# A fused attention and token-mixing kernel on one core: a new written-out order for all five engines

## The chip, the cores and the metric

The kernel runs on one of the eight cores of a Trainium2 chip. A core has five engines that run side by side and meet through semaphores: TensorE (PE) multiplies matrices and writes into PSUM, ScalarE (ACT) and VectorE (DVE) do elementwise work and move results from PSUM to SBUF, GpSimd (POOL) does elementwise work in SBUF and issues DMAs, SyncE (SP) only issues DMAs. PSUM has eight banks per partition; this kernel sees them as four pairs. The metric is device microseconds of one execution, and the number given for a kernel is the median of its runs.

## The reference

Attention with a sliding window of 128 tokens and a bias that falls with distance, and behind it a token-mixing layer whose mixing weights are computed from the tokens themselves:

```python
scores = scale * np.matmul(q, k.transpose(0, 1, 3, 2))        # 8 batches, 8 heads, 576 tokens, 64 wide
mask = (rel >= 0) & (rel < window)
scores = np.where(mask, scores + bias[None], -1000000000.0)
attn = softmax(scores)
x = (attn @ v).transpose(0, 2, 1, 3).reshape(B, S, H * D)     # 8 x 576 x 512
wq = x @ w_q
wk = x @ w_k
W_tok = scale * np.einsum('bsd,btd->bst', wq, wk)
mixed = np.einsum('bst,btd->bsd', W_tok, x)
out = np.maximum(mixed, 0.0) @ w_out
```

## The kernel before

**Stages of a batch.** The kernel works through eight batches. For each batch, loads bring in q, k and v and turn them to 16 bits on the way (`Lq`, `Lk`, `Lv`, with `Lt` for the last 64 tokens of two batches together). TensorE transposes q and k (`TW` for batches 0 to 3, `TN` for 4 to 7, `TT` for the last tokens), and ACT or DVE copies each transposed block out of PSUM (`ETW`, `ETN`, `ETT`). Then follow, for four groups of keys and two halves of the heads each, the scores (`QK`), their exponential on ACT (`EXP`, 64 in all), and the multiplication by the precomputed exponential of bias and mask on DVE (`MUL`, 64 in all). `PV` multiplies by v, and `X` on DVE divides by the row sums (a reciprocal and a multiplication; 40 in all). The token mixing transposes x (`XT`, copied by `EXT`), projects it (`WQ`, `WK`, copied by `EWQ`, `EWK`), forms x transposed times wk (`G`, copied by `EG`), mixes (`MX`, copied through the ReLU by `RM`), and multiplies by w_out (`OUT`, copied by `EO`, stored by `DO`). `mixed` is computed as wq times (wk transposed times x), so no 576 by 576 matrix is formed.

**The order.** Nothing of the order follows from loops. The functions of the kernel only register operations with their dependencies. A string `ORDER` then lists all 773 operations, each with its engine: `QK0.2.0:P:1:5` stands for the scores of batch 0, group 2, half 0 on PE (`P`), in PSUM pair 1, behind 5 fill matmuls; a second digit of a bank names the half of the pair; `A`, `V`, `G` and `S` are ACT, DVE, POOL and SP. The loop at the end of the kernel (lines 861 to 876) emits the operations in that order. Each engine runs its own operations strictly in the order of the string, so what counts is the order within an engine; between engines, and for the reuse of a PSUM bank, semaphores make one wait for the other. A fill matmul computes nothing that is used; it multiplies a constant tile into a bank that the next operation overwrites.

**The load queue.** All loads but the first two run through POOL's queue, in which set-up work (`iota`, `mask`, `ident`, and memsets such as `ones`, `zerop`, `pads`) and part of the stores stand too. `load` (line 368) gives each load an estimated service time; before a load is issued, it waits for an earlier one to have landed, so that the estimated service of the loads under way stays within `AHEAD`, 6.0 us. `HOLD` marks a place in SP's list: the first store of SP behind it waits for the load that is the fourth from the last to have landed.

**What a PE operation waits for** can be read from the names: `TW` needs its loads and the permutation matrix `permh` (`perm`, made from `ident`); `QK` needs the copies of both transposes of its half; `PV` needs the `MUL` of its groups and its v; every one of them needs its bank to have been emptied by the copy behind the operation that had the bank before.

Of the kernel before, what the change touches and what calls it, by code (L numbers as in the profile page):

```python
# [44 lines left out]
ETT0:A MUL0.0.1:V QK0.3.0:P:1:2 ETT1:V EXP0.3.0:A Lv0.3:G PV0.0:P:2 MUL0.1.1:V QK0.3.1:P:3  # L45
X0.0:V ETW1.1.0:A Lv0.4:G PV0.2:P:1 ETW1.1.1:A Lk2.1:G MUL0.3.0:V PV0.1:P:2 EXP0.3.1:A
X0.2:V Lk2.0:G QK1.2.1:P:0 EXP1.2.1:A QK1.1.1:P:3 MUL0.3.1:V Lq2.1:G TW1.0:P:1:1 X0.1:V
EXP1.1.1:A Lq2.0:G PV0.3:P:0 ETW1.0.0:A MUL1.1.1:V Lwq:G QK1.3.1:P:2 ETW1.0.1:A X0.3:V
PV0.4:P:3 EXP1.3.1:A QK1.0.1:P:1 X0.4:V Lv1.0:G XT0.0:P:0 EXP1.0.1:A EXT0.0:V Lv1.1:G
XT0.2:P:20:2 QK1.2.0:P:3 QK1.0.0:P:1 EXT0.2:A MUL1.0.1:V EXP1.2.0:A XT0.1:P:0 Lwk:G  # L50
QK1.1.0:P:2 MUL1.3.1:V EXP1.0.0:A EXT0.1:V Lv1.2:G TW2.1:P:3 MUL1.2.0:V EXP1.1.0:A Lv1.3:G
MUL1.2.1:V QK1.3.0:P:0 ETW2.1.1:A TW2.0:P:1 MUL1.0.0:V Lt1.2:G ETW2.1.0:A wqq:V EXP1.3.0:A
Lv1.4:G MUL1.1.0:V WQ0.0:P:20 ETW2.0.0:V PV1.0:P:3 Lt1.3:G ETW2.0.1:A WQ0.1:P:21 X1.0:V
EWQ0.0:A Lt1.1:G QK2.1.1:P:0 EWQ0.1:A QK2.0.0:P:1 Lwo.0:G PV1.1:P:2 MUL1.3.0:V EXP2.0.0:A
WK0:P:30 Lt1.0:G X1.1:V EXP2.1.1:A WQ0.2:P:31 PV1.2:P:1 Lk3.0:G EWQ0.2:V QK2.1.0:P:2 EWK0:A
ones4:G X1.2:V PV1.3:P:0 EXP2.1.0:A QK2.0.1:P:3 Lq3.0:G X1.3:V PV1.4:P:1 EXP2.0.1:A
QK2.2.0:P:2 Lwo.1:G X1.4:V G0:P:00 EXP2.2.0:A Lwo.3:G XT1.0:P:3 ones2:G EG0:V XT1.2:P:01
XT1.1:P:1 EXT1.0:A EXT1.2:V QK2.2.1:P:2 EXT1.1:V TT1:P:0 Lwo.2:G MX0.0:P:3 ETT3:A MUL2.0.1:V
Lv2.0:G WQ1.1:P:10 ETT2:A EXP2.2.1:A RM0.0:V WK1:P:11 ones3:G EWQ1.1:V WQ1.0:P:01 RM0.2:A
EWK1:V QK2.3.0:P:2 EWQ1.0:A Lv2.1:G MUL2.2.0:V MX0.2:P:3 MX0.1:P:1 G1:P:00 RM0.4:A  # L60
MUL2.1.1:V RM0.3:A Lk3.1:G TW3.0:P:3 EXP2.3.0:A EG1:V Lv2.2:G MUL2.2.1:V QK2.3.1:P:0 RM0.1:A
MX1.0:P:2 ETW3.0.1:V Lq3.1:G EXP2.3.1:A MX1.1:P:1 MUL2.0.0:V OUT0.1:P:31 Lv2.4:G RM1.0:A
RM1.1:V Lv2.3:G PV2.0:P:0 RM1.3:A ETW3.0.0:V OUT0.0:P:20 RM1.2:A X2.0:V Lq4.0:G EO0.1:A
OUT0.2:P:10 EO0.0:A MUL2.1.0:V QK3.0.0:P:3 MUL2.3.1:V Lq4.1:G QK3.1.0:P:0 EO0.2:A PV2.1:P:2
MUL2.3.0:V EXP3.0.0:A Lv3.0:G OUT1.0:P:11 X2.1:V EXP3.1.0:A Lq4.2:G PV2.2:P:3 MUL3.0.0:V
TW3.1:P:2 EO1.0:A Lk4.3:G MUL3.1.0:V X2.2:V QK3.2.0:P:0 ETW3.1.0:A Lk4.1:G PV2.4:P:1
EXP3.2.0:A ETW3.1.1:V OUT0.3:P:20 Lk4.0:G X2.4:V QK3.2.1:P:3 Lk4.2:G QK3.0.1:P:0 EO0.3:V
EXP3.2.1:A PV2.3:P:1 Lq4.3:G OUT1.3:P:21 EXP3.0.1:A X2.3:V Lv3.1:G WQ1.2:P:20 QK3.3.1:P:3
EWQ1.2:A EO1.3:V QK3.3.0:P:1 EXP3.3.1:A XT2.1:P:0 Lt2.3:G MUL3.2.1:V OUT1.2:P:20 Lv3.2:G
EXP3.3.0:A EXT2.1:V XT2.2:P:21 XT2.0:P:3 MUL3.0.1:V TN4.0.0:P:0 Lv3.4:G EXT2.2:A EXT2.0:A  # L70
MX1.2:P:1 WQ2.1:P:21 ETN4.0.0:V Lv3.3:G RM1.4:A QK3.1.1:P:3 MUL3.2.0:V EWQ2.1:A TN4.1.0:P:1
EXP3.1.1:A PV3.0:P:0 Lt2.0:G MUL3.3.1:V OUT1.4:P:21 Lv4.0:G X3.0:V ETN4.1.0:A TN4.0.1:P:3
EO1.2:A TN4.1.1:P:1 MUL3.1.1:V Lq5.3:G QK4.0.1:P:0 ETN4.0.1:A WK2:P:20 EO1.4:V ETN4.1.1:A
Lt2.2:G PV3.1:P:3 EXP4.0.1:A MUL3.3.0:V Lq5.2:G QK4.0.0:P:1 X3.1:V WQ2.0:P:21 EXP4.0.0:A
# [18 lines left out]
Lv5.4:G MUL5.3.0:V WQ3.2:P:21 WQ4.0:P:30 EXP5.2.0:A Lk7.1:G EWQ3.2:V WQ4.1:P:31 EG4:V
EWQ4.0:V MX3.2:P:0 TN6.0.1:P:2 EWQ4.1:A Lk7.3:G TN6.1.1:P:1 RM3.4:V ETN6.0.1:A XT5.0:P:3
ETN6.1.1:V TT3:P:0 Lv6.2:G EXT5.0:A QK6.1.1:P:2 MUL5.2.0:V MX4.0:P:1 ETT6:A MX4.1:P:3
EXP6.1.1:A Lv7.3:G RM4.0:V OUT3.4:P:00 RM4.1:V RM4.3:A Lv6.1:G PV5.3:P:2 RM4.2:A MUL6.0.1:V
QK6.0.0:P:3 EO3.4:A Lv6.0:G PV5.2:P:1 X5.3:V ETT7:A OUT4.2:P:00 EXP6.0.0:A Lq7.2:G X5.2:V
QK6.1.0:P:2 Lq7.3:G QK6.2.1:P:3 MUL6.0.0:V EXP6.1.0:A TN7.1.0:P:1 OUT4.3:P:01 EO4.2:V
DO3.4:G EXP6.2.1:A ETN7.1.0:V PV5.4:P:2 MUL6.1.1:V QK6.3.0:P:1 EO4.3:A Lk7.2:G TN7.0.0:P:3
X5.4:V EXP6.3.0:A OUT4.1:P:00 Lv6.3:G MUL6.1.0:V ETN7.0.0:A QK6.3.1:P:2 XT5.1:P:1 MUL6.3.0:V  # L100
DO0.0:G EXP6.3.1:A QK6.2.0:P:3 OUT3.3:P:01 EO4.1:V Lv7.1:G EXT5.1:A MUL6.2.1:V PV6.0:P:2
EXP6.2.0:A DO2.2:G OUT4.0:P:00 X6.0:V Lv6.4:G EO3.3:A WQ5.1:P:10 MUL6.2.0:V EO4.0:A DO0.1:G
XT5.2:P:11 TN7.0.1:P:3 TN7.1.1:P:2 EWQ5.1:A EXT5.2:V QK7.0.0:P:0 ETN7.0.1:V DO2.3:G
ETN7.1.1:A PV6.2:P:1 MUL6.3.1:V EXP7.0.0:A DO1.0:G WQ5.0:P:30 X6.2:V PV6.1:P:2 Lv7.4:G
EWQ5.0:A QK7.1.1:P:0 QK7.1.0:P:3 X6.1:V Lv7.0:G EXP7.1.1:A WQ4.2:P:10 WK5:P:11 HOLD:S
EWQ4.2:V DO3.3:G PV6.4:P:2 EXP7.1.0:A EWK5:V QK7.2.0:P:0 DO1.1:G X6.4:V PV6.3:P:1 EXP7.2.0:A
DO0.3:G QK7.3.1:P:3 X6.3:V G5:P:20 EXP7.3.1:A DO4.2:G XT6.0:P:0 EG5:V DO1.2:G XT6.1:P:1
EXT6.0:A XT6.2:P:21 QK7.0.1:P:3 EXT6.1:V EXT6.2:A Lv7.2:G EXP7.0.1:A MX5.1:P:0 MX4.2:P:2
WQ6.0:P:10 RM5.3:V DO3.0:G WK6:P:11 RM5.1:A MUL7.3.1:V RM4.4:A WQ5.2:P:30 DO1.4:G
QK7.2.1:P:0 EWQ5.2:A MUL7.0.0:V MX5.0:P:2 EWK6:A QK7.3.0:P:3 EWQ6.0:V RM5.0:A G6:P:11  # L110
RM5.2:V DO3.2:G EXP7.3.0:A WQ6.1:P:10 MUL7.1.0:V DO2.0:G OUT5.2:P:20 EG6:A EWQ6.1:V
EXP7.2.1:A MUL7.1.1:V OUT5.3:P:21 MUL7.3.0:V EO5.2:A MX6.1:P:1 MUL7.2.0:V MX5.2:P:3
MX6.0:P:0 EO5.3:A OUT5.1:P:20 RM5.4:V RM6.1:A MUL7.0.1:V RM6.3:A PV7.4:P:3 MUL7.2.1:V
RM6.2:A PV7.1:P:1 EO5.1:A X7.4:V OUT5.0:P:21 RM6.0:A DO5.1:G X7.1:V PV7.0:P:3 PV7.3:P:0
EO5.0:A X7.0:V WQ6.2:P:20 PV7.2:P:1 DO5.0:S OUT6.2:P:21 X7.3:V DO2.1:S OUT6.1:P:30 DO1.3:S
X7.2:V EO6.2:A EWQ6.2:A XT7.2:P:31 XT7.0:P:0 DO6.2:S EO6.1:V EXT7.2:A XT7.1:P:1 MX6.2:P:2
# [793 lines left out]
```

## Time and profile before

| | us |
|---|---|
| median of 3 runs | 137.87 (137.78 to 138.77) |
| the profiled execution, span from the first to the last instruction | 137.4 |
| PE busy | 127.2 (93% of the span) |
| ACT busy | 113.8 (83%) |
| DVE busy | 112.0 (82%) |
| POOL busy | 105.3 (77%) |
| end of the last matmul | 132.45 |

The profiled execution has no time of its own beside its span; its span of 137.4 stands 0.5 below the median of the runs, which is what lies around it. Matmuls are pipelined: a row's duration runs until the result is in PSUM, and the next operation starts before that. So the cost of a PE operation is read from its start to the start of the next one.

### The profile page before, as it was taken

To read this page: it belongs to the slowest core of one execution; us is meant where nothing else is said; L and a number is where in the kernel's file an instruction comes from. 1 tells how busy PE (TensorE), PEld (TensorE's weight loads), DVE (VectorE), ACT (ScalarE), POOL (GpSimd) and SP (SyncE) were. 2 spreads that over 40 slices of the span, in tenths; PEclk is the share of its full clock that TensorE was granted. 3 is DMA by queue.
4 is the path that set the end of the run, shared out by engine and by line. 5 is a ranking of instruction groups with operands and counts; after the bars stand their busy time and mean duration, and the time that the engine had idled before them with its cause. 6 is when DMAs were issued, how large, how long until landed. Compare 5 with 4: busy or idle time off the path is not lost.

```text
span 137.4 us, 5570 instructions
## 1 busy us (share of the span) xinstructions
PE 127.2 (93%) x2364; PEld 83.5 (61%) x2364; DVE 112.0 (82%) x236; ACT 113.8 (83%) x187; POOL 105.3 (77%) x170
## 2 busy tenths in 40 slices
...
DMA packets 92680, 24.86 MB, mean 181 GB/s; under 512 B 80240, under 2 KB 89200, under 8 KB 92656
## 3 DMA queue, kind: packets, MB, share of 16 engines
...
q8 instruction: 18, 0.29, 0.8%
...
## 4 chain that ended last, share of the span: by engine, by line
PE 72%; ACT 8%; DMA 5%; POOL 5%; issue 3%; DVE 2%; POOLq 0%; DVEq 0%
PE pair L214 62%; PE pair L217 10%; DMA natw<-in_k_dram 5%; ACT pt L604 5%; POOL natt L220 2%; POOL natw L220 2%; ACT qkT L492 2%; DVE x L650 1%; DVE xtl L650 1%; DVE xT L237 1%; DVE inv L649 0%; ACT xT L235 0%; ACT osb L229 0%; ACT wqT L229 0%; POOL wm L293 0%
## 5 line engine op out<-in xcount | busy, mean ns | idle before, releaser
L604 ACT ACTIVATE pt<-pair 128x1024 f16<-128x1024 f32 x64 | 63.3, 1038 | 6.0 <-PE pair L214 5.8
L220 POOL DMA_DIRECT2D vt<-in_v_dram x40 | 36.5, 968 | 1.2 <-DMA natw<-in_k_dram 0.8
L611 DVE TENSOR_TENSOR pt<-pt,bias 128x1024 f16<-128x1024 f16 x48 | 32.2, 684 | 1.4 <-ACT pt L604 1.3
L214 PE MATMUL pair<-wout_sb,rm 128*128 128x512 f16 x128 | 32.0, 380 | 0.1
L223 POOL DMA_DIRECT2D out_dram<-natw x19 | 10.6, 566 | 19.5 <-DVE natw L231 10.9
L214 PEld LDWEIGHTS <-pt 128*128 128x128 f16 x576 | 21.2, 98 | 5.5 <-issue 2.2
L214 PE MATMUL pair<-qkT 64*128 64x256 f16 (+3 forms) x352 | 23.8, 247 | 0.4 <-ACT pt L604 0.3
L214 PE MATMUL pair<-vt,pt 128*128 128x65 f16 x576 | 23.8, 194 | 0.1
L220 POOL DMA_DIRECT2D natw<-in_k_dram x24 | 22.9, 993 | 1.2 <-POOLq L894 0.8
L220 POOL DMA_DIRECT2D natw<-in_q_dram x23 | 21.5, 989 | 2.0 <-DMA natw<-in_k_dram 0.7
L650 DVE TENSOR_TENSOR x<-pair,inv 128x512 f16<-128x512 f32 x32 | 22.1, 692 | 1.1
L214 PEld LDWEIGHTS <-rm 128*128 128x128 f16 x128 | 10.8, 97 | 10.9 <-issue 0.9
L214 PEld LDWEIGHTS <-qkT 64*128 64x128 f16 x352 | 11.9, 96 | 7.7 <-issue 3.9
L229 ACT COPY natw<-pair 128x512 f32<-128x512 f32 x24 | 14.1, 607 | 2.2 <-PE pair L214 2.1
L217 PEld LDWEIGHTS <-natw 128*64 128x64 f16 (+1 forms) x512 | 12.8, 103 | 4.8 <-issue 1.9
L214 PE MATMUL pair<-fill 128*128 128x512 f16 x28 | 10.4, 506 | 1.2 <-DVE fill L348 1.2
L750 ACT ACTIVATE rm<-pair 128x512 f16<-128x512 f32 x20 | 11.4, 611 | 0.0
L611 DVE TENSOR_TENSOR pt<-pt,biasl 128x1024 f16<-128x1024 f16 x16 | 10.9, 683 | 0.0
L217 PE MATMUL pair<-permh,natw 128*64 128x128 f16 x256 | 9.1, 223 | 1.8 <-DMA natw<-in_k_dram 1.4
L649 DVE RECIPROCAL inv<-pair 128x8 f32<-128x8 f32 (+1 forms) x40 | 8.1, 203 | 3.1 <-PE pair L214 2.3
L214 PE MATMUL pair<-xT,wqq_sb 128*128 128x256 f16 x64 | 9.3, 273 | 0.4 <-ACT qkT L492 0.4
L752 DVE TENSOR_SCALAR rm<-pair 128x512 f16<-128x512 f32 x12 | 7.9, 684 | 1.6 <-PE pair L214 1.6
...
## 6 DMA issues: line engine op xcount, KB each, us to landing
...
```

The lines of the kernel that those rows point to most:

```text
L214: hold(nc.tensor.matmul(*a, **k))
L217: hold(nc.tensor.transpose(*a))
L220: hold(nc.gpsimd.dma_start(**k))
L223: i = (nc.gpsimd if eng == "POOL" else nc.sync).dma_start(**k)
L229: hold(nc.scalar.copy(out_ap, in_ap))
L492: hold(nc.scalar.copy(dst, src))
L604: nc.scalar.activation(out=pt[:, 0:1024], in_=two(s.bank).rearrange("p e c -> p (e c)"), func=AF.Exp, scale=SCALE)
L611: nc.vector.tensor_tensor(out=pt[:, 0:1024], in0=pt[:, 0:1024], in1=bt, op=ALU.mult)
L649: nc.vector.reciprocal(out=inv[r], in_=pxv[r, :, :, 64])
L650: nc.vector.tensor_tensor(out=x[r].rearrange("p (g h d) -> p g h d", g=2, h=4), in0=pxv[r, :, :, 0:64], in1=inv[r].unsqueeze(3).broadcast_ ...
L750: hold(nc.scalar.activation(out=out_ap, in_=in_ap, func=AF.Relu, scale=WSCALE))
L752: hold(nc.vector.tensor_scalar(out=out_ap, in0=in_ap, scalar1=0.0, scalar2=WSCALE, op0=ALU.max, op1=ALU.mult))
```

## The change

Only the string `ORDER` differs. The same 773 operations stand in it. What differs:

- the order within every engine, from the first operation to the last;
- which of ACT and DVE does a copy out of PSUM: ACT has 5 `ETT` fewer, 2 `ETN` fewer, 2 short `EWQ` and 2 short `EXT` fewer, 3 `EXT`, 2 `EG`, 1 `EWK`, 1 `EWQ` and 1 `EO` more, and DVE the opposite;
- the memsets: `zerop`, `pads` and `ones4` move from POOL to DVE, `ones0` from DVE to POOL;
- the fill matmuls: 10 ahead of the first transposition, where there were 28 at eight places (12, 5, 1, 3, 2, 2, 1 and 2);
- the PSUM bank of most PE operations;
- the stores: POOL has 20 and SP 16, where each had 18, and `HOLD` stands three places before the end of the string.

The beginning and the end of the string, before (`-`) and after (`+`):

```diff
 ORDER = """
-FQ1:S ones1:V FQ0:S Lk0.0:G ones0:V iota:G Lq0.1:G dist:V mask:G Lk0.1:G bias1:A ident:G
-CQ0:V CQ1:A Lt0.2:G zeros:V bias0:A idh:V Lt0.1:G perm:V TW0.0:P:0:12 Lt0.0:G biasl0:V
-Lq1.1:G ETW0.0.1:A ETW0.0.0:V Lt0.3:G QK0.2.0:P:1:5 Lk1.1:G QK0.1.0:P:2 EXP0.2.0:A Lv0.0:G
-TW0.1:P:0:1 EXP0.1.0:A Lv0.2:G QK0.0.0:P:3 ETW0.1.1:V ETW0.1.0:A zerop:G MUL0.1.0:V
-EXP0.0.0:A QK0.2.1:P:1:3 QK0.0.1:P:2 QK0.1.1:P:0 MUL0.0.0:V Lv0.1:G EXP0.1.1:A TT0:P:3
-biasl1:V Lk1.0:G EXP0.2.1:A MUL0.2.0:V Lq1.0:G TW1.1:P:0:2 EXP0.0.1:A MUL0.2.1:V pads:G
...
-EO7.4:A OUT7.0:P:00 DO7.4:S EO7.1:V OUT7.3:P:01 DO7.1:G EO7.0:A OUT7.2:P:10 DO7.0:S EO7.3:A
-DO7.3:S EO7.2:A DO7.2:S
+FQ0:S FQ1:S zerop:V pads:V Lk0.1:G Lq0.1:G Lk0.0:G iota:G Lt0.2:G dist:V ones4:V Lq1.0:G mask:G
+bias1:A bias0:A ones0:G ident:G biasl1:V CQ1:A perm:V TW0.1:P:0:10 Lt0.3:G Lt0.1:G Lt0.0:G
+zeros:V CQ0:V TW0.0:P:1 ETW0.1.0:A ETW0.1.1:A QK0.1.1:P:0 EXP0.1.1:A QK0.0.1:P:2 QK0.2.1:P:3
+ETW0.0.1:V ETW0.0.0:V EXP0.0.1:A QK0.2.0:P:1 EXP0.2.0:A biasl0:V MUL0.1.1:V Lk1.0:G QK0.0.0:P:0
+EXP0.0.0:A QK0.1.0:P:2 EXP0.1.0:A Lv0.0:G EXP0.2.1:A ones1:V idh:V TT0:P:1 MUL0.0.1:V ETT0:V
+QK0.3.0:P:0 EXP0.3.0:A Lv0.1:G ETT1:V MUL0.2.0:V MUL0.1.0:V Lk1.1:G MUL0.0.0:V TW1.0:P:1
+QK0.3.1:P:2 PV0.0:P:3 X0.0:V PV0.1:P:0 Lq1.1:G ETW1.0.0:A ETW1.0.1:A QK1.2.0:P:1 QK1.0.0:P:3
...
+EXP2.1.0:A TW2.1:P:1 ETW2.1.1:V ETW2.1.0:A MUL1.3.0:V XT1.0:P:2 EXT1.0:A PV1.2:P:3 X1.2:V
...
+EXP2.2.0:A TW3.1:P:1 ETW3.1.0:A TT1:P:0 WQ1.2:P:20 ETT2:A MUL2.1.1:V MUL2.1.0:V MUL2.0.1:V
+ETW3.1.1:V MUL2.2.1:V MUL2.2.0:V MUL2.0.0:V EWQ1.2:V ETT3:V WK1:P:30 EWK1:A QK2.3.1:P:1
+EXP2.3.1:A QK2.3.0:P:3 EXP2.3.0:A MUL2.3.1:V G1:P:00 EG1:A QK3.0.1:P:1 EXP3.0.1:A TW3.0:P:2
...
+EO7.3:A DO7.4:S DO7.3:S OUT6.3:P:31 DO6.0:G EO7.1:A DO7.1:S OUT7.2:P:30 EO7.2:V EO6.3:A DO6.3:S
+DO7.2:S OUT6.2:P:20 EO6.2:V OUT7.0:P:31 EO7.0:A HOLD:S DO6.2:S DO7.0:S
 """
```

More of the change, by code (lines that the diff above doesn't have):

```diff
@@ L45 @@
[L45 to L74, printed above, removed]
@@ L93 @@
[L93 to L116, printed above, removed]
```

89 lines of the change are left out of this document (67 added, 22 removed).

## The prediction

> **What bounds the kernel now.** I read the page first, then the busy times in stretches of 10 us, then PE's timeline.
>
> ```profile
> span 137.4 us, 5570 instructions
> PE 127.2 (93%) x2364; PEld 83.5 (61%) x2364; DVE 112.0 (82%) x236; ACT 113.8 (83%) x187; POOL 105.3 (77%) x170
> PE 72%; ACT 8%; DMA 5%; POOL 5%; issue 3%; DVE 2%; POOLq 0%; DVEq 0%
> ```
>
> ```profile
> 10.00:20.00 10.00, 7.69 (x129) 4.56 (x124) 5.97 (x12) 6.73 (x10) 9.43 (x23) 0.84 1.77 165
> 20.00:30.00 10.00, 9.32 (x243) 7.51 (x244) 9.47 (x19) 9.99 (x15) 7.40 (x10) 0.99 1.59 165
> 40.00:50.00 10.00, 10.00 (x175) 6.51 (x173) 9.91 (x20) 9.85 (x17) 9.09 (x12) 1.00 1.90 156
> 120.00:130.00 10.00, 10.00 (x120) 5.53 (x118) 5.97 (x13) 5.33 (x13) 0.54 (x1) 1.00 0.94 340
> ```
>
> The columns of the second view are stretch, length, then busy time of PE, weight loads, DVE, ACT and POOL, and PE's granted clock, DMA share, GB/s. PE holds 72% of the chain of waits and is full from 40 us on, but DVE and ACT are nearly full beside it (9.91 and 9.85 of 10): three engines in balance. Slack exists only in the first 40 us and, for DVE and ACT, behind 120. To see what PE can still save I need the price of its operations, from start to next start:
>
> ```profile
> 42.24 1.06 PE L217 MATMUL pair<-permh,natw 128*64 128x128 f16 x32
> 43.24 0.41 PE L214 MATMUL pair<-qkT 64*128 64x128 f16 x12
> 43.48 0.74 PE L214 MATMUL pair<-wqT,gs 64*128 64x512 f16 x4
> 44.20 1.02 PE L214 MATMUL pair<-wout_sb,rm 128*128 128x512 f16 x4
> 45.06 0.42 PE L214 MATMUL pair<-vt,pt 128*128 128x65 f16 x8
> ...
> 128.83 3.62 PE L214 MATMUL pair<-wout_sb,rm 128*128 128x512 f16 x16
> ```
>
> A TW costs 43.24 - 42.24 = 1.00, a QK 0.24, an OUT 0.86, and so on; an operation behind one of another array tiling costs 0.10 more. These are PE's first rows from TW3.0 on and its last, the end, 128.83 + 3.62 = 132.45. With the median step of each kind between them, the 256 PE operations cost 112.9 us in the order of before (108 changes of tiling). So 132.45 - 112.9 = 19.6 us are lost. TW3.0 starts at 42.24 with 24.4 us of work ahead of it: 17.8 lost by then, 1.8 in the 90 us behind. **The change is decided by what PE loses before 44 us, and by whether the rest stays gapless.**
>
> **The change part by part.**
>
> *PE work.* In the new order the same sum is 112.5 us (111 changes of tiling, but fewer in front of costly kinds). 18 fills less save nothing: they stand where PE would wait. *ACT and DVE.* ACT hands eleven mostly short copies to DVE and takes eight longer ones: within 0.2 us on either engine; zerop, pads and ones4 run on DVE in its first 6 us, where it waits for the mask anyway.
>
> *The start.* These rows carry it:
>
> ```profile
> 1.28 0.90 POOL L220 DMA_DIRECT2D natw<-in_k_dram  x1 [0.83 <-POOLq L894]
> 4.28 1.33 ACT L305 ACTIVATE bias<-wm 128x256 f16<-128x256 f32 x4 [2.26 <-POOL wm L295]
> 5.36 0.29 POOL masks.py:199 TENSOR_SCALAR_AFFINE_SELECT ident<-ident 128x128 f32<-128x128 f32 x1
> 6.42 1.15 PE L217 MATMUL pair<-permh,natw 128*64 128x128 f16 x32
> 7.66 0.80 POOL L220 DMA_DIRECT2D natw<-in_q_dram  x1
> 8.69 0.63 PE L214 MATMUL pair<-qkT 64*128 64x256 f16 x8
> 9.14 1.94 ACT L604 ACTIVATE pt<-pair 128x1024 f16<-128x1024 f32 x2 [0.93 <-PE pair L214]
> 11.62 1.00 POOL L336 MEMSET pt<- 128x64 f16 x10
> 15.25 1.01 POOL L340 MEMSET xtl<- 128x512 f16 x2
> 16.29 1.03 PE L217 MATMUL pair<-permh,natw 128*64 128x128 f16 x24 [1.40 <-DMA natw<-in_k_dram]
> 18.87 1.02 ACT L604 ACTIVATE pt<-pair 128x1024 f16<-128x1024 f32 x1 [3.18 <-PE pair L214]
> ```
>
> Before, ident is ready at 5.36 + 0.29 = 5.65, the first TW starts at 6.42, the first EXP at 9.14. In the new order POOL issues five loads (0.8 each, as at 7.66) and iota, mask and ones0 ahead of ident: ident is ready near 7.8. On DVE, perm stands behind biasl1, which waits for bias1 on ACT, which waits for the mask (6.5) and takes 1.33, as at 4.28: bias1 to 7.85, biasl1 to 8.5, perm to 8.7. First TW at 8.7, 2.3 later; the first EXP at about 11.9, 2.8 later.
>
> Against that stands a stall that goes: before, ACT waits 3.18 us until 18.87, because PE's TW1.1 sits until 16.29 on a load and QK0.3.0 stands behind it. The new order puts QK0.3.0 ahead of TW1.0. Eight EXP at 0.91 (steps below) from 11.9, with two ETW between, end at 20.2 where before they end at 21.8. POOL also loses the memsets at 11.62 and 15.25 (2.5 us with the short ones behind). Summing POOL's new order, each load lands at least 1 us ahead of its use up to 44 us, so what is late next is an eviction, not a load. PE reaches the first QK of batch 1 at 19.35 with 6.1 us done: 13.2 lost, against 14.4 before.
>
> *20 to 44 us.* From here I walked the new order by hand, with these steps:
>
> ```profile
> 19.79 1.07 ACT L492 COPY qkT<-pair 128x512 f32<-128x512 f32 x2
> ...
> 26.79 2.85 ACT L604 ACTIVATE pt<-pair 128x1024 f16<-128x1024 f32 x3
> ...
> 28.45 1.88 DVE L611 TENSOR_TENSOR pt<-pt,bias 128x1024 f16<-128x1024 f16 x3
> ...
> 34.79 0.69 DVE L650 TENSOR_TENSOR x<-pair,inv 128x512 f16<-128x512 f32 x1
> ...
> 35.72 0.69 DVE L650 TENSOR_TENSOR x<-pair,inv 128x512 f16<-128x512 f32 x1
> ```
>
> ETW on ACT 0.48 (1.07 less the last one's 0.59), EXP 0.91 ((2.85 - 1.03) / 2), MUL 0.60 ((1.88 - 0.68) / 2), X 0.93 (35.72 - 34.79), a QK's result after 0.45 (8.69 to 9.14). The gain melts, because DVE has its copies behind runs of MUL. ETW2.1.1 stands behind X1.1, MUL1.2.1 and RM0.1: QK2.1.1 waits until 35.8 and ACT idles 0.8. ETW3.1.1 stands behind three MUL: QK2.3.1 waits until 41.9. EWQ1.2, behind three more, frees the bank of TW3.0 only at 43.8. Landmarks of PE's lost time (before in brackets, at the same work done): TW2.1 at 33.4, 16.2 (17.1); TW3.1 at 39.4, 17.1 (17.7); TW3.0 at 43.85, 17.9 (17.8). DVE and ACT are by then 1.0 and 0.3 us further than before with their own work.
>
> *The fills and the clock.* PE's granted clock, by the same columns as above:
>
> ```profile
> 13.30:16.71 3.41, 1.58 (x32) 0.95 (x33) 2.97 (x7) 2.40 (x4) 3.06 (x8) 1.00 2.12 160
> 16.71:20.13 3.42, 3.40 (x54) 2.14 (x50) 1.05 (x3) 1.26 (x2) 3.07 (x5) 0.52 1.73 179
> ...
> 26.95:30.37 3.42, 2.98 (x98) 2.49 (x93) 3.42 (x7) 3.42 (x5) 3.35 (x5) 1.00 1.90 139
> ```
>
> ```profile
> 18.22 0.61 PE L214 MATMUL pair<-qkT 64*128 64x128 f16 x12
> ...
> 24.10 0.41 PE L214 MATMUL pair<-qkT 64*128 64x128 f16 x12
> ```
>
> One stretch of 3.4 us in which PE was busy 46% (1.58 of 3.41) was followed by one at half clock, in which 12 matmuls took 0.61 instead of 0.41; a stretch of 87% was not. Without fills PE has about 2.8 us of work in 11.4 to 20 us, a third, so I take that time at half clock, and PE about 80% busy at full clock behind it, between the two rows. Bounds: nothing if the clock holds from 20 us (half clock before is in the walk); if it stays half until 44, the 19.8 us of work between 19.35 and 43.85 grow by a third to a half (1.03 for 24 transposes at 16.29 against 1.06 for 32 at 42.24, and 0.61 to 0.41), 6.6 to 10 us, of which the 5 us of waits there cover most: about 4 net. I take 0.7: about six results in 20 to 28 us that ACT and DVE wait for, 0.1 later each. This is nearer the lower row because a PE slowed down is busy all the time, which at 16.71 gave the clock back after one stretch.
>
> [...]
>
> *From 44 us to the end.* Loads are early here. The evictions are tighter: PE work between an operation and the next on its bank is 2.10 us in the mean (2.18 before), and under 1.5 in 85 of 322 reuses (56 of 316); result and EXP alone take 0.45 + 1.04. The run PV2.1, PV2.0, PV2.3, PV2.4, each needing the X of two before, alone costs 1.1. From below, the waits vanish (-1.8); from above, three times before's (+3.6). I take +1.3, that run and a little for the rest: 3.1 instead of 1.8. At the end PV7.2 leaves 14.9 us of PE work (13.1 before), with OUT4 to OUT6 as filler: no gap over 0.3.
>
> *Stores.* The last one goes as before:
>
> ```profile
> 132.49 0.59 ACT L229 COPY osb<-pair 128x512 f32<-128x512 f32 x1 [0.28 <-PE pair L214]
> ```
>
> 137.4 - 132.45 = 4.95 behind the last matmul, the same after, since DO7.0 is again a single store behind ACT's last copy. HOLD at the end lets DO2.2 and DO0.3 go among the loads; the other SP stores queue behind DO4.2, whose copy comes near 113 us, when loads are over.
>
> *Sum.* Lost: 17.9 + 0.7 + 3.1 = 21.7. Last matmul 112.5 + 21.7 = 134.2, span 139.15. The median of before is 0.5 above its profiled span, so **139.6 us**, 1.3% slower.
>
> **The rivals.**
>
> *A: the early lead is kept.* If the copies slip in 0.3 to 0.5 us earlier than I walked, DVE's and ACT's lead of 0.3 to 1.0 becomes PE's: lost 16.4 at 44, then 1.8: 112.5 + 18.2 + 4.95 + 0.5 = 136.1. For it: the 1.6 us that ACT is ahead at 20. Against: DVE as the bound of 20 to 44, 9.47 of 10 already before.
>
> *B: no change.* Walk right, clock warm from 20 us, the rest as before: 17.9 + 1.8 lost, 112.5 + 19.7 + 4.95 + 0.5 = 137.6. Against it stand the tighter banks and the missing fills; for it, that DVE and ACT are no later than before at 44. [...]
>
> *C: the clock stays half until 44 us.* One mechanism, PE between 19 and 44 us, deciding once its busy share there falls under a point that lies between 46% and 87%: lost 17.9 + 4 + 3.1 = 25.0, 143.0.
>
> *D: the order does not take hold.* Engines run strictly in order, so nothing reorders it; I give it nothing.
>
> **How the numbers follow.** Forecast 0.38, A 0.24, B 0.23, C 0.15. The range runs from half a us under A to the price of C, 135.6 to 143.0, and leaves out the far sides of both, some 0.08 each. A measurement of this kernel tells about 1% from no change (136.5 to 139.25). Faster: A but for its slow edge, 0.22. Same: that edge, B and the lower two fifths of the forecast, 0.40. Slower: the rest of the forecast and C, 0.38.
>
> **What would show it.** Right: first TW near 8.7 and first EXP near 11.9; no wait of ACT of 3 us; half clock in 10 to 20 us; TW3.0 near 44.5; DVE and ACT over 9.4 of 10 from 25 to 110 with short waits of PE on evictions; 4.9 us behind the last matmul. Wrong: TW3.0 before 43, or PE gapless from there (A); a clock under 0.8 in 20 to 40 us (C); a wait of PE on a load, or a gap of PE over 1 us behind 60 us, which I have no term for.

## The result, and the profile after

| | us |
|---|---|
| median before, beside the runs after | 138.32 (137.78 to 140.26) |
| median after, 4 runs | 142.38 (141.69 to 142.90) |
| ratio | 1.0279, 95% interval 1.0211 to 1.0347 |
| the profiled execution after: time, span | 142.73, 140.6 |
| end of the last matmul | 136.49 (before 132.45) |

The new order is 2.8% slower; the ratio is formed from the faster executions of each kernel, so it is not the quotient of the two medians. First the page of the kernel after, the span, the busy times and the first line of its chain of waits:

```profile
span 140.6 us, 5554 instructions
PE 125.1 (89%) x2346; PEld 85.4 (61%) x2346; DVE 112.8 (80%) x253; ACT 114.0 (81%) x184; POOL 103.6 (74%) x158
POOL 41%; PE 28%; DMA 15%; issue 5%; DVE 5%; ACT 3%; POOLq 0%; ACTq 0%
```

All three engines have a smaller share of a longer span. The chain now names POOL, but it is followed back from the end through whatever released last, and in the early part it runs down the load queue. Whether PE waits for loads is asked of the view of waits instead: what PE waited for between 20 and 130 us, with total, count and the longest one. Before:

```profile
PE pair L217 <- ACT pt L604: 0.4, 1, 0.4
PE pair L214 <- ACT qkT L492: 0.4, 1, 0.4
PE pair L214 <- ACT pt L604: 0.3, 1, 0.3
PE pair L214 <- DVE xtl L650: 0.3, 1, 0.3
```

After (line numbers are lower by 4, since the string is shorter):

```profile
PE pair L210 <- ACT qkT L231: 1.7, 2, 1.0
PE pair L210 <- DVE qkT L490: 0.8, 2, 0.6
PE pair L210 <- DVE x L646: 0.6, 3, 0.3
PE pair L213 <- DVE x L646: 0.5, 1, 0.5
...
```

Before has four waits, 1.4 us in all. After has nine rows, 4.7 us in all, and no row names a DMA: no wait of PE there is put down to a load, although the chain runs through the load queue. The largest row is new: PE waits twice, up to 1.0 us, for ACT's copy of transposed q and k at L231. The same stretches as in the prediction, of the kernel after (columns as there):

```profile
20.00:30.00 10.00, 8.76 (x214) 7.16 (x213) 9.24 (x21) 9.12 (x12) 8.29 (x16) 0.94 1.74 169
40.00:50.00 10.00, 9.33 (x232) 7.22 (x232) 9.37 (x20) 9.33 (x16) 9.71 (x14) 1.00 1.97 159
80.00:90.00 10.00, 9.02 (x207) 6.25 (x203) 8.62 (x17) 9.31 (x16) 10.00 (x15) 1.00 1.99 177
100.00:110.00 10.00, 9.32 (x186) 6.55 (x184) 7.80 (x17) 8.53 (x17) 6.39 (x11) 1.00 1.29 276
120.00:130.00 10.00, 10.00 (x168) 6.46 (x165) 8.51 (x19) 4.85 (x11) 2.79 (x6) 1.00 0.79 263
```

In 40 to 50 PE is busy 9.33 where it was 10.00. In 80 to 90 and 100 to 110 it has gaps while DVE (8.62, 7.80) has room: that points to waits rather than to a lack of engine time.

The lost time of the prediction (start of a PE operation less the PE work ahead of it, at the same prices) says where it comes from. One profiled execution each, at 0, 8, 24, 40 and 112 us of PE work done; the experiments are explained below:

| kernel | 0 | 8 | 24 | 40 | 112 |
|---|---|---|---|---|---|
| before | 6.4 | 15.2 | 17.8 | 18.0 | 19.4 |
| after | 8.6 | 15.7 | 18.9 | 20.4 | 23.8 |
| e1_fills | 9.8 | 15.9 | 19.2 | 20.6 | 24.1 |
| e2_no_fills | 6.3 | 14.0 | 16.9 | 18.6 | 20.1 |
| e3_head_before | 6.4 | 13.2 | 23.3 | 29.6 | 32.8 |
| e4_head_after | 8.6 | 14.5 | 17.8 | 22.0 | 23.8 |
| e5_no_wait | 9.1 | 15.7 | 19.1 | 20.5 | 22.1 |
| e6_before_no_wait | 6.0 | 13.2 | 16.0 | 16.8 | 17.7 |
| e7_qk_ahead | 6.1 | 14.9 | 17.6 | 17.7 | 19.2 |
| e8_copies_first | 8.8 | 15.6 | 18.6 | 21.2 | 24.3 |
| e9_start | 6.4 | 14.6 | 17.9 | 19.8 | 21.5 |
| e10_after_again | 8.9 | 14.6 | 18.1 | 21.1 | 22.9 |
| e11_before_again | 5.8 | 14.1 | 17.1 | 18.6 | 21.1 |
| e12_short_exp | 9.3 | 16.2 | 19.1 | 20.2 | 21.7 |

A profiled execution can lie 1 us off the median of its kernel: that of e6_before_no_wait took 1.2 us less, those of e2_no_fills, e10_after_again and e11_before_again 1.0 to 1.3 us more.

After against before: 0.4 us more by 8 us of work, 0.7 more by 24, 1.3 more by 40, 2.0 more behind that. The column at 8 needs care: kernels with the same head differ by 2 us at 8 (13.2 to 15.2), so a difference there is read from means, not from two executions.

### The profile page after: what moved, and what is told of

It reads as the page before. It is cut to its first block, busy times and chain, and to the rows that moved or that the text cites. A ratio compares the mean times of both kernels' runs of the same rounds, so it can differ in the third digit from the quotient of the medians.

```text
span 140.6 us, 5554 instructions
## 1 busy us (share of the span) xinstructions
PE 125.1 (89%) x2346; PEld 85.4 (61%) x2346; DVE 112.8 (80%) x253; ACT 114.0 (81%) x184; POOL 103.6 (74%) x158
## 4 chain that ended last, share of the span: by engine, by line
POOL 41%; PE 28%; DMA 15%; issue 5%; DVE 5%; ACT 3%; POOLq 0%; ACTq 0%
PE pair L210 26%; POOL natw L216 18%; POOL vt L216 12%; DMA natw<-in_k_dram 7%; POOL natt L216 6%; DMA natw<-in_q_dram 4%; DMA vt<-in_v_dram 4%; POOL wout_sb L216 2%; PE pair L213 2%; DVE x L646 1%; POOL vt L319 1%; DVE pt L607 1%; ACT qkT L231 1%; ACT pt L600 1%; DVE inv L645 1%
## 5 line engine op out<-in xcount | busy, mean ns | idle before, releaser
L216 POOL DMA_DIRECT2D vt<-in_v_dram x40 | 37.1, 984 | 4.3 <-DMA vt<-in_v_dram 1.9
L607 DVE TENSOR_TENSOR pt<-pt,bias 128x1024 f16<-128x1024 f16 x48 | 31.4, 682 | 0.1
L210 PE MATMUL pair<-qkT 64*128 64x256 f16 (+3 forms) x352 | 24.3, 252 | 3.7 <-ACT qkT L231 1.7
L219 POOL DMA_DIRECT2D out_dram<-natw x22 | 12.5, 595 | 19.0 <-ACT natw L225 14.1
L210 PEld LDWEIGHTS <-pt 128*128 128x128 f16 x576 | 21.2, 99 | 6.7 <-issue 3.3
L210 PE MATMUL pair<-vt,pt 128*128 128x65 f16 x576 | 24.1, 195 | 0.7 <-DVE x L646 0.6
L216 POOL DMA_DIRECT2D natw<-in_k_dram x24 | 23.8, 1018 | 1.2 <-POOLq L890 0.8
L646 DVE TENSOR_TENSOR x<-pair,inv 128x512 f16<-128x512 f32 x32 | 22.1, 692 | 1.1
L216 POOL DMA_DIRECT2D natw<-in_q_dram x23 | 22.3, 1023 | 0.5 <-DMA natw<-in_k_dram 0.5
L213 PEld LDWEIGHTS <-natw 128*64 128x64 f16 (+1 forms) x512 | 14.8, 113 | 7.0 <-DMA natw<-in_q_dram 4.0
L210 PEld LDWEIGHTS <-qkT 64*128 64x128 f16 x352 | 13.2, 97 | 9.2 <-issue 3.5
L225 ACT COPY natw<-pair 128x512 f32<-128x512 f32 x26 | 15.1, 601 | 3.5 <-PE pair L210 3.4
L213 PE MATMUL pair<-permh,natw 128*64 128x128 f16 x256 | 10.7, 251 | 3.8 <-DVE permh L282 3.7
L746 ACT ACTIVATE rm<-pair 128x512 f16<-128x512 f32 x20 | 11.9, 616 | 1.0 <-PE pair L210 0.9
L233 DVE COPY qkT<-pair 128x1024 f16<-128x1024 f16 (+1 forms) x14 | 7.8, 568 | 1.0 <-ACT natw L225 0.5
```

Source lines behind the costliest of these rows:

```text
L210: hold(nc.tensor.matmul(*a, **k))
L213: hold(nc.tensor.transpose(*a))
L216: hold(nc.gpsimd.dma_start(**k))
L219: i = (nc.gpsimd if eng == "POOL" else nc.sync).dma_start(**k)
L225: hold(nc.scalar.copy(out_ap, in_ap))
L233: hold(nc.vector.tensor_copy(out=out_ap, in_=in_ap))
```

## The experiments

**Clock and fills.** e1_fills puts fills back into the kernel after (41 in all: the 28 that its expectation names are those of before), e2_no_fills takes those behind the first transposition from before:

```diff
-TW0.1:P:0:10
+TW0.1:P:0:27
-QK0.0.0:P:0
+QK0.0.0:P:0:3
-QK0.1.0:P:2
+QK0.1.0:P:2:3
...
```

> The kernel after, with 28 fill matmuls where there were 10: 27 ahead of the first transposition and 3, 3, 3, 2, 2, 1 ahead of QK0.0.0, QK0.1.0, TT0, QK0.3.0, TW1.0, QK0.3.1. Everything else as after. Theory 1 (the loss is made of copies that stand behind other work on ACT and DVE, and of the PSUM banks that they free late): the half clock costs at most the 0.7 us that the prediction gave it, so 141.7 us beside 142.4 of the kernel after, 1.024 of the kernel before. Rival 1 (the missing fills and the half clock in the first 21 us make most of the loss): 139.5 us or less, 1.01 of the kernel before or less, and the first QK of batch 1 more than 1 us ahead of its 20.92. Rival 2 (the new early order itself makes the loss, whatever the clock): as Theory 1.

```diff
-QK0.2.0:P:1:5
+QK0.2.0:P:1
-TW0.1:P:0:1
+TW0.1:P:0
...
```

> The kernel before without its 16 fill matmuls behind the first transposition (the 12 ahead of it stay). Theory 1: the clock falls for some microseconds in 8 to 20 us and that costs 0.3 to 1 us, so 138.6 to 139.3 us. Rival 1: the fills are worth most of the 4 us between the two kernels, so 141 us or more. Rival 2: no more than 1 us, as Theory 1.

Measured: e1_fills 142.84 us, 1.0303 of before (1.0239 to 1.0368); e2_no_fills 138.72, 0.9998 (0.9956 to 1.0041). The stretch from 10 to 20 us, first of the kernel after, then of e1_fills:

```profile
10.00:20.00 10.00, 8.56 (x149) 6.49 (x145) 6.18 (x18) 8.23 (x11) 8.49 (x12) 0.67 1.83 168
```

```profile
10.00:20.00 10.00, 9.47 (x174) 5.50 (x169) 6.05 (x18) 8.14 (x11) 8.30 (x12) 1.00 1.81 160
```

The clock goes from 0.67 to 1.00 and nothing is gained: ACT and DVE did the same work in those 10 us (8.23 and 8.14; 6.18 and 6.05). Rival 1 falls as far as the missing fills go. What the half clock alone costs is not shown, since the fills delay PE too: the first transposition starts at 9.79 instead of 8.63. e2_no_fills cannot tell it either. The same stretch there:

```profile
10.00:20.00 10.00, 6.81 (x143) 5.41 (x144) 6.81 (x14) 7.82 (x12) 9.33 (x23) 0.83 1.72 162
```

The granted clock is 0.83 without the 16 fills and 0.84 in the kernel before with them. So they did not hold the clock up, and taking them away tests only the fills, which are worth nothing.

**Head and tail.** e3_head_before takes the order of before up to TW3.0 and that of after from there on; e4_head_after the reverse:

```diff
 MX0.1:P:1 G1:P:00 RM0.4:A MUL2.1.1:V RM0.3:A Lk3.1:G
-TW3.0:P:3 EXP2.3.0:A EG1:V Lv2.2:G MUL2.2.1:V QK2.3.1:P:0
...
+Lq3.1:G Lv2.2:G RM0.1:V Lv2.3:G TW3.1:P:1 ETW3.1.0:A WQ1.2:P:20
...
```

> The order of before up to TW3.0 (some 42 us), the order of after from there to the end. Theory 1: PE loses 17.8 us up to TW3.0 as before, then the 4.7 us that the kernel after loses behind it instead of 1.8: 138.3 + 2.9 = 141.2 us. Rivals 1 and 2 (all of the loss is made in the head, by the clock or by the order): 138.3 us, 1.00 of the kernel before.

```diff
 G1:P:00 EG1:A QK3.0.1:P:1 EXP3.0.1:A
-TW3.0:P:2 ETW3.0.0:V ETW3.0.1:A MUL2.3.0:V MX1.2:P:0
...
+Lwo.0:G Lwo.2:G WQ1.1:P:10 EWQ1.1:V TW3.0:P:3 MX1.0:P:2
...
```

> The order of after up to TW3.0, the order of before from there to the end. Theory 1: 19.3 us lost up to TW3.0 as in the kernel after, then 1.8 as before: 138.3 + 1.5 = 139.8 us, or less, if the tail of before takes up part of it. Rivals 1 and 2: 142.4 us, 1.03 of the kernel before.

Measured: 150.32 us, 1.0826 (1.073 to 1.0923), and 145.18, 1.0471 (1.0391 to 1.055). All theories missed, because the seams are expensive. The first row is PE at the seam of e3_head_before, the second of e4_head_after:

```profile
47.72 1.92 PE L214 MATMUL pair<-permh,natw 128*64 128x128 f16 x32 [6.51 <-DMA natw<-in_q_dram]
```

```profile
45.87 1.01 PE L211 MATMUL pair<-xT,wqq_sb 128*128 128x256 f16 x4 [1.70 <-ACT pt L601]
```

In e3_head_before TW3.1 stands directly behind the seam, and its load Lq3.1, which the queue of before issues only behind TW3.0, goes out there too: PE is idle for 6.51 us. So the times of the two kernels say nothing. What lies behind the seam does: from 40 us of work on, the tail of after loses 3.1 us behind the head of before (29.64 to 32.77) and 3.4 in the kernel after, the tail of before 1.7 behind the head of after (22.04 to 23.78) and 1.5 in its own kernel. About 1.4 to 1.9 us of the loss belong to the tail, whatever stands ahead of it. Rival 2 falls for that part.

**The two waits.** PE and ACT in the kernel after where the tail loses most (start, duration, in brackets the idle time and its releaser):

```profile
87.16 0.41 PE L213 MATMUL pair<-identh,natw 64*128 64x64 f16 x16
87.77 0.71 ACT L231 COPY qkT<-pair 128x512 f32<-128x512 f32 x1
88.54 0.61 PE L210 MATMUL pair<-qkT 64*128 64x256 f16 x8 [0.98 <-ACT qkT L231]
...
106.97 0.58 ACT L231 COPY qkT<-pair 128x512 f32<-128x512 f32 x1
107.61 0.61 PE L210 MATMUL pair<-qkT 64*128 64x256 f16 x8 [0.68 <-ACT qkT L231]
```

At 87.16 PE transposes (TN6.0.1), ACT copies (ETN6.0.1), and QK6.0.0, next on PE, starts 0.06 us behind the end of that copy; from start to start that costs 1.14 us more than the price of the transposition. At 107.61 QK7.0.1 stands likewise behind ETN7.1.1 (0.85 us). But QK6.0.0 does not need this copy. ETN6.0.1 writes columns 256 to 511 of q, QK6.0.0 reads columns 0 to 255, and it is registered with ETN6.0.0 and ETN6.1.0 alone:

```python
need = [evt[b, 1, g // 2]] + [evt[b, 0, m] for m in sorted({g // 2, min(g + 1, 3) // 2})]
```

Both copies write into the same tile of SBUF that the QK reads. e5_no_wait keeps the order of after, and declares for every QK that the other copies of its batch are no dependency, except those that free its bank; e6_before_no_wait is the same edit of before:

```diff
         keep = [i for d in op.deps for i in d.insts]
+        if op.group and op.banks:
+            keep += [i for d in rank if d.frees and d.insts and d.frees[0].bank[0] == op.bank[0] for i in d.insts]
...
-        s = add(f"QK{b}.{g}.{u}", pe(0.228), need, em, banks=2, mode=1)
+        s = add(f"QK{b}.{g}.{u}", pe(0.228), need, em, banks=2, mode=1, group=f"q{b}")
```

> The kernel after in the same order, but QK6.0.0, QK7.0.1 and every other QK is told that it does not depend on the copies of its own batch other than those that it is registered with (their columns of the transposed tile are not the ones it reads). Theory 1 (two waits that the order does not know of, QK6.0.0 for ETN6.0.1 and QK7.0.1 for ETN7.1.1, are the loss of 75 to 108 us): the two rows of 1.14 and 0.85 us go, PE loses 1.5 us from 75 us on instead of 3.4, and the time is 140.4 us, 1.014 of the kernel before. Rival 3 (the PSUM banks and the fullness of ACT and DVE are the limit there, and PE would wait for something else): the lost time comes back within 10 us, 142 us or more, 1.026.

> The kernel before with the same edit. Theory 1: its order has no QK directly behind a copy of its own batch that it does not read, so nothing changes, 138.3 us, within 0.4. Rival 3: the edit shortens the waits of all kernels alike, so it gains here as much as in the kernel after.

Measured, with the kernel before at 139.18 us beside both: e5_no_wait 140.85 us, 1.0133 (1.0083 to 1.0183), so half of the 2.8% is gone; e6_before_no_wait 138.70, 0.9944 (0.9901 to 0.9988). PE and ACT of e5_no_wait at the same place, and the first row of its waits of PE between 20 and 130 us:

```profile
87.28 0.41 PE L213 MATMUL pair<-identh,natw 64*128 64x64 f16 x16
87.52 0.60 PE L210 MATMUL pair<-qkT 64*128 64x256 f16 x8
```

```profile
87.90 0.71 ACT L231 COPY qkT<-pair 128x512 f32<-128x512 f32 x1
```

```profile
PE pair L210 <- DVE qkT L492: 1.2, 3, 0.6
```

QK6.0.0 now starts at 87.52, before the copy begins at 87.90, and the row of 1.7 us is gone from the waits. The lost time behind 40 us of work is 1.6 instead of 3.4, and it does not come back later: Rival 3 falls. The edit also frees the copies from the QK of their batch, but no wait of ACT or DVE for such a QK stands in the profile after between 20 and 130 us. In the order of before the QK that follows such copies (QK6.1.1 behind ETN6.1.1) has two PE operations between; there the edit gains 0.6%, at the edge of what can be told, against 1.5% here. Theory 1 expected nothing, and the profiles cannot credit the edit with it: behind 8 us of work e6_before_no_wait loses 4.5 us, before 4.2, and the lower loss ahead of that (13.2 against 15.2) e3_head_before shows without the edit. Why an order between disjoint columns is kept at all was not examined further.

**The stall that goes.** e7_qk_ahead makes, in before, the one step of the change that was to free ACT of its 3.18 us:

```diff
-TW1.1:P:0:2 EXP0.0.1:A MUL0.2.1:V pads:G ETT0:A MUL0.0.1:V QK0.3.0:P:1:2
+EXP0.0.1:A MUL0.2.1:V pads:G ETT0:A MUL0.0.1:V QK0.3.0:P:1:2 TW1.1:P:0:2
```

> The kernel before with QK0.3.0 ahead of TW1.1 on PE, which is the step of the change by which the prediction takes ACT's wait of 3.18 us away. If that wait is worth time: the first EXP behind it starts 2 us earlier, PE loses 0.5 to 1 us less by 24 us, 137.3 us, 0.993 of the kernel before. If loads (TW1.1, TW1.0) and DVE set the pace there: within 0.3 us of the kernel before.

Measured: 139.15 us, 1.0001 (0.9968 to 1.0033). ACT in e7_qk_ahead:

```profile
16.23 1.02 ACT L601 ACTIVATE pt<-pair 128x1024 f16<-128x1024 f32 x1 [0.59 <-PE pair L211]
19.05 1.07 ACT L489 COPY qkT<-pair 128x512 f32<-128x512 f32 x2 [1.80 <-PE pair L214]
```

The EXP starts at 16.23 instead of 18.87, and then ACT waits 1.80 us for the transposition TW1.1, which had stood ahead of it. The wait moved by one instruction. In the order of before the step is worth nothing.

**Copies behind MULs.** e8_copies_first moves three copies of the kernel after forward on DVE:

```diff
-ETT2:A MUL2.1.1:V MUL2.1.0:V MUL2.0.1:V ETW3.1.1:V MUL2.2.1:V MUL2.2.0:V MUL2.0.0:V EWQ1.2:V ETT3:V
+ETT2:A ETW3.1.1:V ETT3:V MUL2.1.1:V MUL2.1.0:V MUL2.0.1:V EWQ1.2:V MUL2.2.1:V MUL2.2.0:V MUL2.0.0:V
```

> The kernel after with three copies moved ahead of MULs on DVE: ETW3.1.1 and ETT3 ahead of MUL2.1.1, EWQ1.2 ahead of MUL2.2.1. The step of the prediction under test is that the gain melts in 20 to 44 us because DVE has its copies behind runs of MUL. If it is right: QK2.3.1 and TW3.0 come 0.4 to 0.7 us earlier and the 1.3 us that PE loses between 24 and 32 us of its work become 0.6; 141.7 us. If DVE's and ACT's amount of work is the limit there, whatever its order: no gain, 142.4 us or up to 0.5 more.

Measured: 142.93 us, 1.0282 (1.0238 to 1.0327). PE of e8_copies_first:

```profile
43.09 0.41 PE L211 MATMUL pair<-qkT 64*128 64x128 f16 x12
...
48.50 0.40 PE L211 MATMUL pair<-qkT 64*128 64x256 f16 x4 [0.73 <-DVE qkT L491]
```

QK2.3.1 comes 0.3 us earlier than in the kernel after (43.38 there), but TW3.0 does not (45.49, there 45.31), and 0.73 us are lost at 48.50 on a copy that is now later (47.76, there 46.43): DVE stood idle for 1.35 us ahead of the first moved copy, until 42.12, and the MULs come behind it. The step "the gain melts, because DVE has its copies behind runs of MUL" named a wait that is there, but moving these copies moves the wait and saves nothing.

**The start.** e9_start gives e5_no_wait the start of before:

```diff
-FQ0:S FQ1:S zerop:V pads:V Lk0.1:G Lq0.1:G Lk0.0:G iota:G Lt0.2:G dist:V ones4:V Lq1.0:G mask:G
-bias1:A bias0:A ones0:G ident:G biasl1:V CQ1:A perm:V TW0.1:P:0:10 Lt0.3:G Lt0.1:G Lt0.0:G
+FQ0:S FQ1:S zerop:V pads:V Lk0.0:G Lq0.1:G Lk0.1:G iota:G CQ0:V dist:V mask:G ident:G Lt0.2:G
+ones4:V Lq1.0:G CQ1:A bias0:A bias1:A ones0:G perm:V biasl0:V TW0.0:P:0:10 Lt0.3:G Lt0.1:G Lt0.0:G
...
```

> The kernel of e5_no_wait with the two halves of batch 0 swapped, as the kernel before has them: TW0.0 first, whose q comes through SP (CQ0, CQ1 early), so that it needs only one load of POOL's queue; iota, mask and ident behind the first three loads, perm ahead of biasl0. Theory 2 (what is left of the loss is, for 1.3 us, the start: the kernels with the head of before lose 13.2 to 15.2 us by 8 us of PE's work, mean 14.1, those with the head of after 14.5 to 15.9, mean 15.5): first TW at 6.7 instead of 9.0, 1.2 us less lost by 8 us of work and at the end, 139.6 us, 1.004 of the kernel before. Rival 4 (the loads set the pace behind the first TW, so the lead melts by 20 us): 140.8 us as e5_no_wait, 1.013.

Measured: 140.37 us, 1.0106 (1.0063 to 1.0149), between the two. PE of e9_start:

```profile
6.35 1.92 PE L214 MATMUL pair<-permh,natw 128*64 128x128 f16 x32 [0.71 <-DVE permh L285]
...
10.00 1.49 PE L214 MATMUL pair<-permh,natw 128*64 128x128 f16 x24 [0.73 <-DMA natw<-in_k_dram]
```

```profile
45.44 0.69 PE L214 MATMUL pair<-permh,natw 128*64 128x128 f16 x17 [0.52 <-issue]
```

The first TW is 2.7 us earlier than in e5_no_wait, the second is broken up by loads, and 1.1 us of lead are left at 8 and at 24 us of work. Then TW3.0 stops half way for 0.52 us, with nothing in the profile that it waited for, and 0.6 us of lead reach the end; in the medians it is 0.3%, inside the intervals. A start as before's was expected to bring 1.2; half of that is in the profile, and the medians cannot tell it from nothing.

**What is left in the middle.** Between 16 and 32 us of PE work e5_no_wait still loses 2.7 us (17.68 to 20.35), before 0.8. e12_short_exp takes work from ACT and DVE there:

```diff
+        wide = 256 if b in (2, 3) else 1024
...
-            nc.scalar.activation(out=pt[:, 0:1024], in_=two(s.bank).rearrange("p e c -> p (e c)"),
+            nc.scalar.activation(out=pt[:, 0:wide], in_=two(s.bank).rearrange("p e c -> p (e c)")[:, 0:wide],
...
-            nc.vector.tensor_tensor(out=pt[:, 0:1024], in0=pt[:, 0:1024], in1=bt, op=ALU.mult)
+            nc.vector.tensor_tensor(out=pt[:, 0:wide], in0=pt[:, 0:wide], in1=bt[:, 0:wide], op=ALU.mult)
```

> The kernel of e5_no_wait in which EXP and MUL of batches 2 and 3 (16 each) work on 256 of their 1024 columns and leave the others out; everything else as there. It prices the amount of work of ACT and DVE between about 33 and 57 us, where PE loses 2.7 us between 16 and 32 us of its own work (17.68 to 20.35). Theory 3 (ACT and DVE have too much to do there for what PE has): with some 9 us less on ACT and 6 us less on DVE that loss falls under 1 us, and the time to 139.0 us, 1.000 of the kernel before. Rival 6 (single chains set it: a result, its copy and the next use of the bank, whose length the narrower EXP and MUL change little): 1.7 to 2.7 us of the loss stay, 140 to 140.8 us, 1.007 to 1.013.

Measured: 140.38 us, 1.0167 (1.0064 to 1.0271). One stretch, first of e5_no_wait, then of e12_short_exp:

```profile
40.00:50.00 10.00, 9.34 (x229) 7.10 (x227) 9.41 (x19) 9.34 (x16) 9.59 (x13) 1.00 1.93 157
```

```profile
40.00:50.00 10.00, 9.76 (x240) 7.54 (x239) 6.92 (x21) 6.26 (x17) 9.48 (x13) 1.00 1.94 160
```

ACT has 3.1 and DVE 2.5 us less to do in these 10, and PE gains 0.4. Of the 2.7 us, 2.0 stay (18.07 to 20.10), and the time does not fall. Theory 3 falls: the amount of work of ACT and DVE is not what holds PE up here. Rival 6 fits. PE's two largest waits between 20 and 130 us, for DVE's copies of q and k and for its X, make 2.0 us where e5_no_wait has 1.9. But that chains of a result, its copy and the next use of the bank or tile are the cause is argued and not shown: no chain was taken apart, and POOL stays as busy as it was (9.59 and 9.48).

**Other orders.** e10_after_again and e11_before_again move the orders of after and before on by small steps: 53 and 39 copies change between ACT and DVE, 61 and 57 PE operations the bank, 40 and 33 of the 256 PE operations their place, some 70 of POOL's 135 too. Their first words:

```diff
-FQ0:S FQ1:S zerop:V pads:V Lk0.1:G Lq0.1:G Lk0.0:G iota:G Lt0.2:G dist:V ones4:V
+zerop:V zeros:V Lk0.1:G iota:G Lq0.1:G dist:V ident:G perm:V mask:G ones4:V FQ0:S TW0.1:P:2:10
...
```

> The order of after moved on by many small steps on all engines (places, ACT or DVE for a copy, banks), with the edit of e5_no_wait and with TW0.0 first. The stretch from 24 to 32 us of PE's work keeps its operations. Theory 3 (in that stretch the order of after asks more of ACT and DVE for the same work of PE than before's, 42.7 and 40.6 us done at 32 us of PE's work against 41.7 and 39.2, and small moves cannot mend that): the start and 8 to 24 gain 2 us, the 1.3 us between 24 and 32 stay: 138.2 to 139 us, 0.995 to 1.0 of the kernel before. Rival 5 (that loss too is a matter of single waits): it goes, and the time is 137.2 us or less, 0.987.

```diff
-FQ1:S ones1:V FQ0:S Lk0.0:G ones0:V iota:G Lq0.1:G dist:V mask:G Lk0.1:G bias1:A ident:G
+iota:G dist:V FQ1:S ident:G mask:G bias0:A ones0:V CQ1:A idh:V FQ0:S perm:V CQ0:V bias1:A Lk0.0:G
...
```

> The order of before moved on by the same kind of small steps, with the edit of e5_no_wait. If the three engines and the load queue leave room: 1 us less lost in the first 24 us of PE's work, and 0.6 us less PE work by fewer changes of tiling, 136.6 us, 0.987 of the kernel before. If the loads set the start: 0.994, as e6_before_no_wait.

e10_after_again still begins with TW0.1, unlike what its expectation says. Measured: 141.24 us, 1.017 (1.0104 to 1.0235), and 140.71, 1.0116 (1.0052 to 1.018): both slower than before, and no faster than the kernels that they started from with the same edit. None of the times that were expected of them came. Waits of PE between 40 and 55 us in e10_after_again:

```profile
PE pair L213 <- issue: 1.9, 2, 1.4
PE pair L210 <- DVE qkT L492: 0.5, 1, 0.5
```

This execution of e10_after_again took 142.28 us where the other three took 141.2, so the 1.9 us without a named releaser may belong to it alone. PE, ACT and SP in e11_before_again:

```profile
49.75 1.08 PE L213 MATMUL pair<-permh,natw 128*64 128x128 f16 x32 [0.98 <-DMA natw<-in_q_dram]
...
133.50 0.58 ACT L225 COPY osb<-pair 128x512 f32<-128x512 f32 x1 [2.00 <-PE pair L210]
...
134.90 0.54 SPq L219 DMA_DIRECT2D out_dram<-osb  x1
```

In e11_before_again a reordered load queue makes TW3.1 wait 0.98 us, and the stores end 6.7 us behind the last matmul (133.47 to 140.2) instead of 5.0, in an execution 1.3 us above its median. The kernel that beats both is the plain one, e6_before_no_wait, by 0.6% of before and with an interval that ends at 0.9988.

## Why the prediction was right or wrong

139.6 us was predicted, slower by 1.3%, in a range from 135.6 to 143.0; 142.4 came, slower by 2.8%. Direction and range held; the sum was 2.8 us short. Its terms:

| term | predicted | measured |
|---|---|---|
| PE work | 112.5 | 112.5, at the prediction's prices; not measured apart |
| lost up to TW3.0 | 17.9 + 0.7 | 19.4 |
| lost behind TW3.0 | 3.1 | 4.6 |
| last matmul | 134.2 | 136.49 |
| behind the last matmul | 4.95 | 4.1 |
| around the span | 0.5 | 2.1 |
| time | 139.6 | 142.73, median 142.38 |

**Around the span: wrong by 1.6 us.** The profiled span of before was set against the median of other runs. The runs of before in the experiments stand 1.8 above their own spans (137.53 us with 135.7), those of after 2.1 (142.73 with 140.6). So the execution profiled before was one of about 139.2 us (137.4 and 1.8), above the median, and the sum made against it mixed two executions.

**The start: the landmarks right, one term small.** PE's first two TW, its first QK of batch 1, and ACT's first seven EXP after:

```profile
8.63 3.63 PE L213 MATMUL pair<-permh,natw 128*64 128x128 f16 x64 [3.72 <-DVE permh L282]
```

```profile
20.92 0.70 PE L210 MATMUL pair<-qkT 64*128 64x256 f16 x8
```

```profile
12.84 6.52 ACT L600 ACTIVATE pt<-pair 128x1024 f16<-128x1024 f32 x7 [1.18 <-PE pair L210]
```

The first TW was predicted at 8.7, for the reason given (perm), and came at 8.63. The first EXP was predicted at 11.9 and came at 12.84: the two TW took 3.63 us where the sum had about 2. The granted clock was already 0.50 there (8.6 to 12.3 us), and not only from 10 us; that this is the cause is an inference, since 32 transposes took 1.92 us in e9_start too (its row at 6.35), in a stretch, 5 to 10 us, with a granted clock of 1.00. Seven EXP then run in one piece, so ACT's wait of 3.18 is gone as predicted; e7_qk_ahead shows that the same step in the order of before was worth nothing. The first QK of batch 1 comes at 20.92 instead of 19.35.

**20 to 44 us: right in size, its cause not borne out.** TW2.1, TW3.1 and TW3.0 after:

```profile
34.81 1.08 PE L213 MATMUL pair<-permh,natw 128*64 128x128 f16 x32
...
40.87 1.08 PE L213 MATMUL pair<-permh,natw 128*64 128x128 f16 x32
...
45.31 1.08 PE L213 MATMUL pair<-permh,natw 128*64 128x128 f16 x32
```

They were walked to 33.4, 39.4 and 43.85: each is 1.4 or 1.5 late, which is what was late at 20.92 (1.6) already. The walk held from there. The 0.7 for the clock was laid between 20 and 28, where the clock was nearly full (0.94 in 20 to 30); the half clock lay ahead of 20 (0.67 in 10 to 20). How much of the 1.6 it makes is not shown: at full clock (1.00 in 5 to 30 us) e1_fills reaches that QK at 20.84, but behind more fills. That loads land in time was right (no DMA among the waits). That copies behind MULs are the cause did not hold up: moving three of them saved nothing (e8_copies_first).

**From 44 us on: the step that failed.** "I take +1.3 ...: 3.1 instead of 1.8" counted only the reuse of banks. The run of PV2.1 to PV2.4 was put at 1.1, and between 24 and 32 us of work, where it lies, 1.3 are lost (18.93 to 20.22). What it had no term for is two QK that wait for a copy they do not read, 1.14 and 0.85 us of lost time in the kernel after; taken away in e5_no_wait they gave back 1.7 of PE's loss and 1.5% of the time. The list of what would show it wrong had "a gap of PE over 1 us behind 60 us": 88.54 comes to it, with 0.98 us idle and 1.14 lost. It could have been seen in the string, where ETN6.0.1 stands directly ahead of QK6.0.0 and shares its tile. The bound from above, +3.6, held (+2.8).

**Stores: right in kind, 0.85 us off.** After, the last copy is again ACT's, at 136.53:

```profile
134.55 2.92 SPq L219 DMA_DIRECT2D out_dram<-osb  x4
...
136.53 0.58 ACT L225 COPY osb<-pair 128x512 f32<-128x512 f32 x1 [2.00 <-PE pair L210]
```

From there to the end it is 4.1 us, where before has 4.95.

**The rivals.** A (the early lead kept) did not happen: there was no lead at 20 us. B (no change) fails on the tail. C (half clock until 44) did not happen: 0.94 in 20 to 30 us, 1.00 behind. Its time, 143.0, was nearly reached by other means. That the range held is luck to that extent: 142.4 lies inside it because its upper end was the price of C.

So the 4.1 us between the medians (142.38 less 138.32) are, in the profiles: 1.5 at the start (by 8 us of work, the kernels with the head of before, e2_no_fills and e7_qk_ahead among them, have lost 14.1 in the mean, those with that of after 15.6), 0.6 between 8 and 24 (3.3 against 2.7), 3.3 behind 24 (of it 1.7 the two waits, the rest in the middle), 0.3 around the span, less 0.85 at the end and 0.4 of PE work. That makes 4.4, 0.3 too much, which single executions leave open. The split also hangs on the prices: with a flat 0.10 us for each of the 108 and 111 changes of tiling, PE work is 0.3 more than before and not 0.4 less, and the losses from 8 to 24 and behind 24 come out at 0.1 and 3.0 instead of 0.6 and 3.3. (In the profile of before a PV of 16 matmuls takes 0.48 us to the next start in front of an operation of its own tiling and 0.58 in front of one of another, in the median.) Only the two waits are shown by an experiment of their own; of the start, in which the later first TW and the half clock come together, e9_start got back less than half, and the rest is located but not explained.
